# Seven products for eight in the second MoE's input product, with w_in's sums kept in DRAM

## The chip, the cores and the metric

The kernel runs on one core of one Trainium2 chip. The metric is the device time of one execution in microseconds: the median of three runs is 862.21 us before the change (861.88 to 862.39). Lower is better. The engines are named as the profile names them: PE is TensorE (PEld its weight loads), DVE is VectorE, ACT is ScalarE, POOL is GpSimd, and SP is SyncE, which here issues all DMAs.

## The reference, cut to what matters

Causal attention in blocks of 64 over 4 batches, 8 heads and 576 positions gives 2304 tokens of 512 values. Two feed-forward parts follow. All of it is float32.

```python
def _moe_ref(x, w1, w2, w3, w_out):            # x [2304, 512], w1..w3 [512, 768]
    h = np.maximum(np.maximum(x @ w1, x @ w2), x @ w3)
    return (h @ w_out).astype(np.float32)      # [2304, 512], y below

def _moe2_ref(x, w_in, w_out):                 # x = y [2304, 512], w_in [512, 2048]
    h = x @ w_in
    g = h * np.cos(h)
    return (g @ w_out).astype(np.float32)      # w_out [2048, 512]
```

## The kernel before, in words

Every product after the scores is made exact enough by splitting both operands into a high and a low part (`hi` is the value rounded to `fp32r`, `lo` the rest) and adding three products: high by high, high by low, low by high. A weight arrives as int64 words of a float64; `convert` (L526) turns 128x512 of them into the two parts: a DMA of 512 KB into `raw`, two scalings on ACT or DVE, three DVE instructions on `t`, a copy to `hi`, and a subtraction on DVE to `lo`.

**Stages.** The attention of 32 items (batch, half, pair of heads) runs first, with units of the first MoE fed in between (`fill`, `units`). `ahead` (L917), called from item 10 on, converts weights of the second MoE early and keeps the two parts in DRAM (`kept_in`, `kept_out`). After the attention the rest of the first MoE runs alone. Its results `y` go by `hm` tiles to DRAM, and `split_y` (L1016) reads them back and splits them.

**The second MoE** goes over five chunks of tokens (four of 512, one of 256) and 16 column tiles of w_in. `hstage` (L1043) makes one tile of h: 12 matmuls into one PSUM bank `psm` (four blocks of 128 of the inner dimension, three products each), then on DVE a cosine's range reduction in two instructions (`th`), the sine on ACT, a multiplication on DVE, and the split into `gh` (copy on ACT) and `gl` (subtraction on DVE). `ostage` (L1065), two tiles later, multiplies `gh` and `gl` by a tile of w_out into the output banks `po` (up to four, one for each 128 tokens): three matmuls of 512 columns for each. Four banks hold `psm` tiles in this part (two of `ps_m`, two of `ps_h`) and four hold `po`. w_in and w_out stay in SBUF, high and low, from the first chunk on.

**What sets the order.** `Plan` records every operation, prices it, and lists it in time order by its own costs, forward and backward in turn (L309, L389). Each engine then runs its instructions strictly as listed. An operation's `lead` makes it due earlier. Copies and subtractions can be given to more than one engine. Pools are opened and closed as operations: what lies in `wc` and `wk2` (L1038: the tiles of the second MoE's inner work) can be used only after `moe` and `wk` are closed, that is when every user of the first MoE's tiles is done, the DMA of the last `hm` to DRAM among them. All of it is recorded by one helper, so every instruction has the line L214 in the profile; the names of the tiles tell them apart.

Of the kernel before, what the change touches and what calls it, by code (L numbers as in the profile page):

```python
# [8 lines left out]
F32 = mybir.dt.float32  # L9
# [120 lines left out]
class Plan:  # L130
# [176 lines left out]
    HOLD = {"SP": 20000.0}  # L307

# [158 lines left out]
def fused_kernel(tc, qk, qk4, q1, k1, v2, w1, w2, w3, wout, w_in2, w_out2, out):  # L467
# [58 lines left out]
    def convert(src, hi, lo, pool, bufs):  # L526
# [10 lines left out]
        R.vector.tensor_tensor(i32(t), i32(t), add, ALU.add)  # L537
        R.copy(hi, t)
        R.sub(lo, t, f32(hi))

# [252 lines left out]
    def pv(*its):  # L793
# [119 lines left out]
    NA = 6  # L913
    AHEAD = [("in", fc) for fc in range(NA, NFC)] + [("out", fc) for fc in range(3, NFC - 1, 3)]
    kept = {}

    def ahead():  # L917
        if len(kept) < len(AHEAD) and converted[0] == 4 * NFF:
            kind, fc = AHEAD[len(kept)]
            both = cv.tile([P, 2, 512], F32R, "both", tag="raw", bufs=CVR)  # L920
            convert(w_in2[fc] if kind == "in" else w_out2[:, fc], both[:, 0], both[:, 1], cv, CVR)
            kept[kind, fc] = dram.tile([P, 2, 512], F32, f"kept_{kind}{fc}")
            R.sync.dma_start(kept[kind, fc], f32(both))
# [31 lines left out]
    for n in range(NI + 1):  # L955
# [23 lines left out]
        if n > 9 and n % 3:  # L979
            ahead()  # L980
# [4 lines left out]
    chunks = [(t, min(CH, NT - t)) for t in range(0, NT, CH)]  # L985
# [4 lines left out]
    wih, wil, woh, wol = {}, {}, {}, {}  # L990
    raw_from = [0]

    def conv(kind, fc, pool, src):
        w = pool.tile([P, 2, 512], F32R, f"w_{kind}{fc}")
        if (kind, fc) in kept:
            R.sync.dma_start(f32(w), kept[kind, fc])
        else:
            raw_from[0] += 1
            convert(src, w[:, 0], w[:, 1], (cv, wb)[raw_from[0] % 2], 2)
        return w  # L1000

    def conv_in(fc, pool):
        w = conv("in", fc, pool, w_in2[fc])
        wih[fc], wil[fc] = ([w[:, i, k * P:(k + 1) * P] for k in range(NK)] for i in range(2))

    def conv_out(fc, pool):
        w = conv("out", fc, pool, w_out2[:, fc])
        woh[fc], wol[fc] = w[:, 0], w[:, 1]

    yh, yl = {}, {}  # L1010

    def alloc_y(pool, c, tag):
        yh[c] = [pool.tile([P, CH], F32R, f"yh{tag}_{k}", tag=f"yh{tag}_{k}") for k in range(NK)]
        yl[c] = [pool.tile([P, CH], F32R, f"yl{tag}_{k}", tag=f"yl{tag}_{k}") for k in range(NK)]

    def split_y(c, k):  # L1016
        t0, n = chunks[c]
        raw = cv.tile([P, 512], F32, "t", tag="t", bufs=4)
        for p, frm, to, m in pieces(t0, n):
            R.sync.dma_start(raw[:, to:to + m], y_dram[p][k][:, frm:frm + m])  # L1020
        R.copy(yh[c][k][:, :n], raw[:, :n])
        R.sub(yl[c][k][:, :n], raw[:, :n], f32(yh[c][k][:, :n]))

    alloc_y(wb, 0, "0")
    for k in range(NA):
        if fill:
            fill.pop(0)[1]()
        conv_in(k, wb)
        if k < NK:
            split_y(0, k)  # L1030
        if fill:
            fill.pop(0)[1]()
    while fill:
        fill.pop(0)[1]()
# [4 lines left out]
    wk2 = R.open(moe, name="wk2", bufs=1)  # L1039
    TWO_PI = 2.0 * math.pi  # L1040
    g = {}

    def hstage(c, fc):  # L1043
        n = chunks[c][1]
        ps = bank()[:, :n]
        prods = [(wih[fc], yh[c]), (wih[fc], yl[c]), (wil[fc], yh[c])]
        for k in range(NK):
            with R.unit():
                for i, (w, x) in enumerate(prods):
                    R.tensor.matmul(ps, w[k], x[k][:, :n], start=(k == 0 and i == 0),  # L1050
                                    stop=(k == NK - 1 and i == 2))
        t = wk2.tile([P, CH], F32, "th", tag="t", bufs=3)[:, :n]
        gh = wk2.tile([P, CH], F32R, "gh", tag="gh", bufs=3)[:, :n]
        gl = wk2.tile([P, CH], F32R, "gl", tag="gl", bufs=3)[:, :n]
        R.vector.tensor_scalar(i32(t), ps, 1.0 / TWO_PI, 0.25, ALU.mult, ALU.add)
        R.vector.scalar_tensor_tensor(t, i32(t), -TWO_PI, ps, ALU.mult, ALU.add)
        R.scalar.activation(t, t, AF.Sin, bias=halfpi)
        R.vector.tensor_tensor(t, ps, t, ALU.mult)
        R.copy(gh, t)
        R.sub(gl, t, f32(gh))  # L1060
        g[c, fc] = (gh, gl)

    banks = {}

    def ostage(c, fc):  # L1065
        t0, n = chunks[c]
        gh, gl = g.pop((c, fc))
        for t in range(n // P):
            if fc == 0:
                banks[c, t] = ps_o.tile([P, DM], F32, "po", tag=f"O{t}")  # L1070
            ts = slice(t * P, (t + 1) * P)
            prods = [(gh, woh[fc]), (gh, wol[fc]), (gl, woh[fc])]
            with R.unit():
                for i, (a, w) in enumerate(prods):
                    R.tensor.matmul(banks[c, t], a[:, ts], w, start=(fc == 0 and i == 0),
                                    stop=(fc == NFC - 1 and i == 2))
            if fc == NFC - 1:
                o = wk2.tile([P, DM], F32, "osb", tag="osb", bufs=2)
                R.copy(o, banks[c, t])
                R.sync.dma_start(out[t0 + t * P:t0 + (t + 1) * P, :], o)  # L1080

    LAG = 2
    seq = [(c, fc) for c in range(len(chunks)) for fc in range(NFC)]
    for n in range(len(seq) + LAG):
        if n < len(seq):
            c, fc = seq[n]
            if c == 0:
                conv_out(fc, wc)
                while len(wih) < min(NFC, NA + 1 + fc * (NFC - NA) // (NFC - 2)):
                    conv_in(len(wih), wc)  # L1090
            if fc == 4 and c + 1 < len(chunks):
                alloc_y(*((wk2, c + 1, "1") if c % 2 == 0 else (wb, c + 1, "0")))
            if 8 <= fc < 8 + NK and c + 1 < len(chunks):
                split_y(c + 1, fc - 8)
            hstage(c, fc)
        if n >= LAG:
            ostage(*seq[n - LAG])
    last = ()
    for p in (ps_h, ps_o, wk2, wc, wb, edge, dram, ps_m, cv, const):
        R.close(p, *last)  # L1100
        last = (p,)
# [63 lines left out]
```

## Time and profile before

| what | value |
|---|---|
| median of three runs | 862.21 us |
| profiled execution: span, first to last instruction | 859.3 us |
| PE busy | 852.3 us (99%) |
| DVE busy | 569.0 us (66%) |
| ACT busy | 446.3 us (52%) |
| DMA | 96.91 MB, mean 113 GB/s |

The page gives the profiled execution's span and no other time of it; 2.9 us lie between that span and the median of the runs. Busy times are sums over one engine; an engine that is busy nearly all the time sets the pace, and the others matter where it waits for them. A matmul's duration in these rows is longer than its share of the engine, because matmuls overlap: the distance between the starts of two neighbours is what one costs.

### The profile page before, as it was taken

The page shows a single profiled execution, that of the slowest core. Times are in us where ns is not written, and L with a number is a line of the kernel's source. Part 1 is how long each engine was busy: PE and PEld are TensorE (multiplying, and loading weights), DVE is VectorE, ACT ScalarE, POOL GpSimd, SP SyncE. Part 2 cuts the span into 40 slices and gives each one's busy share as a digit, 9 for nine tenths or more (in the row PEclk, how much of TensorE's full clock was granted, in tenths as well). Part 3 has the DMA queues.
Part 4 walks back from the last instruction along what each step waited for, and adds up shares of the span by engine and source line. Part 5 has one row for each costly group of instructions (what it writes and reads, how often), then busy time and mean ns, then how long its engine had stood idle before and what let it go on. Part 6 is the DMA issues. An engine that isn't in the chain of part 4 may idle for free.

```text
span 859.3 us, 12728 instructions
## 1 busy us (share of the span) xinstructions
PE 852.3 (99%) x4674; PEld 714.3 (83%) x4674; DVE 569.0 (66%) x1157; ACT 446.3 (52%) x1002; POOL 5.6 (1%) x38
## 2 busy tenths in 40 slices
PE   8999999999999999999999999999999999999998
PEld 7788888888888888888899888888888888888897
DVE  7999999569865598358144989455645564555454
ACT  7997999658775598434224444322332232322233
POOL 2000000000000000000000000000000000000000
PEclk9999999999999999999999999999999999999999
DMA  7655666446643367342125811200011001100000
GB/s 274 214 184 180 219 190 207 132 152 211 227 139 120 111 190 231 140 176 92 48 82 182 342 76 37 74 25 0 1 53 47 0 1 39 36 0 1 25 26 25
DMA packets 47006, 96.91 MB, mean 113 GB/s; under 512 B 6240, under 2 KB 18528, under 8 KB 46944
## 3 DMA queue, kind: packets, MB, share of 16 engines
q1 hardware_dynamic: 46944, 96.10, 33.9%
q8 instruction: 37, 0.61, 0.3%
q14 instruction: 25, 0.20, 0.1%
HBM read 75.63 MB, written 20.45 MB: 112 GB/s over the span
## 4 chain that ended last, share of the span: by engine, by line
PE 90%; DVE 6%; ACT 3%; issue 1%; POOL 0%; DVEq 0%; ACTq 0%; POOLq 0%
PE psm L214 55%; PE po L214 23%; PE tb L214 5%; PE X L214 3%; PE SA L214 2%; PE SB L214 2%; DVE top L214 1%; DVE t L214 1%; ACT prob L214 1%; ACT other L214 1%; DVE hm L214 0%; DVE m2high L214 0%; ACT pt L214 0%; DVE wlo L214 0%; DVE qh L214 0%
## 5 line engine op out<-in xcount | busy, mean ns | idle before, releaser
L214 PE MATMUL psm<-yh,w_in 128*128 128x512 f32 (+1 forms) x640 | 194.4, 368 | 0.0
L214 PE MATMUL po<-w_out,gh 128*128 128x512 f32 x576 | 177.6, 390 | 0.0
L214 ACT ACTIVATE th<-th,halfpi 128x512 f32<-128x512 f32 (+1 forms) x80 | 54.5, 682 | 186.3 <-DVE th L214 186.2
L214 PE MATMUL psm<-xhi,whi 128*128 128x512 f32 (+1 forms) x360 | 135.9, 378 | 0.0
L214 PEld LDWEIGHTS psm<-yh,w_in 128*128 128x128 f32 x640 | 117.1, 188 | 20.6
L214 PE MATMUL psm<-xhi,wlo 128*128 128x512 f32 (+1 forms) x360 | 132.9, 369 | 0.0
L214 PE MATMUL psm<-xlo,whi 128*128 128x512 f32 (+1 forms) x360 | 132.8, 369 | 0.0
L214 PEld LDWEIGHTS po<-w_out,gh 128*128 128x128 f32 x576 | 107.1, 188 | 21.4
L214 PE MATMUL psm<-yl,w_in 128*128 128x512 f32 (+1 forms) x320 | 117.7, 368 | 0.0
L214 PE MATMUL po<-w_out,gl 128*128 128x512 f32 x288 | 112.0, 389 | 0.0
L214 DVE TENSOR_SCALAR th<-psm 128x512 int32<-128x512 f32 (+1 forms) x80 | 51.0, 637 | 73.7 <-PE psm L214 67.6
L214 DVE TENSOR_TENSOR th<-psm,th 128x512 f32<-128x512 f32 (+1 forms) x80 | 51.0, 637 | 51.7 <-ACT th L214 51.6
L214 PEld LDWEIGHTS psm<-xhi,wlo 128*128 128x128 f32 x360 | 67.9, 189 | 11.8
L214 PEld LDWEIGHTS psm<-xhi,whi 128*128 128x128 f32 x360 | 67.9, 189 | 9.4 <-ACT kh L214 0.2
L214 PEld LDWEIGHTS psm<-xlo,whi 128*128 128x128 f32 x360 | 68.0, 189 | 8.9
L214 DVE TENSOR_TENSOR gl<-th,gh 128x512 fp32r<-128x512 f32 (+1 forms) x80 | 50.9, 636 | 35.1 <-ACT gh L214 34.3
L214 DVE TENSOR_TENSOR hm<-psm,hm 128x512 f32<-128x512 f32 (+1 forms) x60 | 37.9, 632 | 54.6 <-PE psm L214 49.4
L214 ACT CAST gh<-th 128x512 fp32r<-128x512 f32 (+1 forms) x77 | 44.4, 576 | 55.1 <-DVE th L214 55.1
L214 PEld LDWEIGHTS psm<-yl,w_in 128*128 128x128 f32 x320 | 60.3, 188 | 10.6
L214 PEld LDWEIGHTS po<-w_out,gl 128*128 128x128 f32 x288 | 54.0, 188 | 11.4
L214 PE MATMUL tb<-ident,prob 128*128 128x128 f32 x374 | 53.6, 273 | 1.6 <-ACT pt L214 1.0
L214 ACT COPY pt<-tb 128x512 f32<-128x512 f32 (+3 forms) x88 | 49.7, 586 | 8.1 <-PE tb L214 7.7
(132 smaller groups left out, 1338.3 us busy)
## 6 DMA issues: line engine op xcount, KB each, us to landing
raw<-w SPq DMA_DIRECT2D x18, 512.0 KB, 4.0
raw<-w_in SPq DMA_DIRECT2D x16, 512.0 KB, 4.2
raw<-w_out SPq DMA_DIRECT2D x16, 512.0 KB, 4.8
k<-k SPq DMA_DIRECT2D x24, 288.0 KB, 3.1
vr<-v SPq DMA_DIRECT2D x16, 320.0 KB, 3.9
q<-q SPq DMA_DIRECT2D x20, 256.0 KB, 2.8
kept_in<-both SPq DMA_DIRECT2D x10, 512.0 KB, 3.6
w_in<-kept_in SPq DMA_DIRECT2D x10, 512.0 KB, 7.6
```

The costliest lines, as they stand in the source:

```text
L214: return lambda: getattr(real, method)(*[value(a) for a in args], **{k: value(a) for k, a in kw.items()})
```

## The change

The tokens go in three blocks `s` of two times 384, w_in's column tiles in eight pairs (j, j+8), and the inner dimension in two halves of 256. A stage (s, j) is then a product of a 2x2 by a 2x2 block matrix, and it is made with seven block products for eight (Strassen's algorithm in a form with shared sums). One block product is six matmuls of 384 columns (two blocks of 128 of the inner dimension, three products each).

- **Sums of w_in.** `pair_sums` makes them once on DVE for each pair: four additions or subtractions of 256 columns. `keep_pair` splits four tiles (three of 512 and one of 256 columns) and writes both parts to DRAM. `load_pair` reads them back for every stage, three stages ahead; w_in no longer stays in SBUF. `convert` is cut into `whole` and `split` for this.
- **Sums of y.** `split_y` makes, for each block and each of two k, four sums on DVE and seven splits, into 18 rotating tiles `y0` to `y17`, of which one block uses 14.
- **The stage.** Three PSUM tiles A, Bk and C take the seven products. Between two products into the same tile the value so far is read out, by ACT (`ha`, `hh`) or by additions on DVE (`hu`, `hv`, `ha`); the next product then adds to what is in the bank. `psm` has only the two banks of `ps_m`, because six banks now hold `po`. The cosine part reads h from SBUF.
- **w_out.** Even pairs stay in SBUF, odd ones are loaded for each block. Only tiles 9, 11 and 13 are kept ahead of time.
- **Order.** `ahead` is called from item 17 on and takes whole pairs, and the first eight items' product of probabilities and v gets a lead of 10000 ns.

```diff
+    EARLIER, FIRST_ITEMS = 10000.0, 8
...
             R.unit_op.cost += R.SWITCH
+            if its[0].n < R.FIRST_ITEMS:
+                R.unit_op.lead = R.EARLIER
...
+    def pair_sums(j):
+        x, y = (whole(w_in2[fc], cv, CVR) for fc in (j, j + HALF))
+        a, b = (cv.tile([P, 512], F32, "t", tag="t", bufs=4) for _ in range(2))
+        one, two = slice(0, QUARTER), slice(QUARTER, 2 * QUARTER)
+        R.vector.tensor_tensor(a[:, one], y[:, one], y[:, two], ALU.add)
+        R.vector.tensor_tensor(a[:, two], a[:, one], x[:, one], ALU.subtract)
+        R.vector.tensor_tensor(b[:, one], x[:, one], y[:, one], ALU.subtract)
+        R.vector.tensor_tensor(b[:, two], x[:, two], a[:, two], ALU.subtract)
+        return x, a, b, y[:, two]
+
+    def keep_pair(j):
+        for n, t in enumerate(pair_sums(j)):
+            both = cv.tile([P, 2, 512], F32R, "both", tag="raw", bufs=CVR)[:, :, :t.n]
+            split(both[:, 0], both[:, 1], t)
+            kept["in", j, n] = dram.tile([P, 2, t.n], F32, f"kept_in{j}_{n}")
+            R.sync.dma_start(kept["in", j, n], f32(both))
...
-        if n > 9 and n % 3:
+        if n > 16 and n % 3 and len(AHEAD) > 3:
             ahead()
...
-    ps_h = R.open(ps_x, name="ps_h", bufs=1, space=PSUM, side="right")
-    bank_pools.append((ps_h, 2))
...
+    def split_y(s):
+        parts7 = [[y_tile() for k in range(2)] for _ in range(7)]
+        for k in range(2):
...
+            put(0, r[0, 0])
+            R.vector.tensor_tensor(a, r[0, 1], r[0, 0], *sub)
+            R.vector.tensor_tensor(b, r[1, 1], a, *sub)
+            put(1, b)
+            put(2, r[1, 0])
+            R.vector.tensor_tensor(r[0, 1], r[1, 1], r[0, 1], *sub)
+            put(3, r[0, 1])
+            put(4, a)
+            R.vector.tensor_tensor(r[1, 0], r[1, 0], b, *sub)
+            put(5, r[1, 0])
+            put(6, r[1, 1])
...
+        A, Bk, C = (bank()[:, :TK] for _ in range(3))
+        a, u, v, h = tile("ha"), tile("hu"), tile("hv"), tile("hh")
+        product(0, A, True)
+        R.copy(a, A)
+        product(1, Bk, True)
+        R.vector.tensor_tensor(u, Bk, a, ALU.add)
+        product(2, A, False)
+        R.copy(h, A)
+        product(3, Bk, False)
+        R.vector.tensor_tensor(v, Bk, a, ALU.add)
+        product(4, C, True)
+        R.vector.tensor_tensor(v, C, v, ALU.add)
+        product(5, Bk, False)
+        R.vector.tensor_tensor(a, Bk, a, ALU.add)
+        product(6, C, False)
+        R.vector.tensor_tensor(u, C, u, ALU.add)
+        for f, x, t in ((j, 0, h), (j + HALF, 1, v), (j + HALF, 0, a), (j, 1, u)):
...
+            R.vector.tensor_scalar(i32(c), t, 1.0 / TWO_PI, 0.25, ALU.mult, ALU.add)
+            R.vector.scalar_tensor_tensor(c, i32(c), -TWO_PI, t, ALU.mult, ALU.add)
+            R.scalar.activation(c, c, AF.Sin, bias=halfpi)
+            R.vector.tensor_tensor(c, t, c, ALU.mult)
+            split(gh, gl, c)
...
+            hstage(s, j)
+            if n + 3 < len(seq):
+                pairs[n + 3] = load_pair(n + 3)
+            if n + 1 < len(seq):
+                load_out(*seq[n + 1])
+            if j == HALF - 1 and s + 1 < NS:
+                ys[s + 1] = split_y(s + 1)
```

**Where the order moves.** Three places matter below. In these rows `psm`, `po` and the other names carry a running number, so that two numbers are two tiles.

PE, where the second MoE begins, before: the last w_in product ahead of the first w_out products. Three more tiles of 12 matmuls, into three other banks, stand ahead of these rows, and nothing of the second MoE's w_out.

```order
L214 MATMUL psm_5489<-yl0_3_4859,w_in3_4772 128x512
L214 MATMUL psm_5489<-yh0_3_4846,w_in3_4772 128x512
L214 MATMUL po_5513<-w_out0_5454,gh_5499 128x512 x2
L214 MATMUL po_5513<-w_out0_5454,gl_5507 128x512
L214 MATMUL po_5520<-w_out0_5454,gh_5499 128x512 x2
L214 MATMUL po_5520<-w_out0_5454,gl_5507 128x512
```

PE at the same place after the change: the last matmul of the first MoE, and the first products of stage (0, 0), with `psm_5585` as Bk, `psm_5601` as A and `psm_5647` as C. `pair0` to `pair2` lie in `wb`, `pair3` in `wc`.

```order
L214 MATMUL psm_5536<-hh_5495,vlo5_1946 128x256
L214 MATMUL psm_5585<-y2_5236,pair1_5332 128x384 x3
L214 MATMUL psm_5585<-y3_5374,pair1_5332 128x384 x3
L214 MATMUL psm_5601<-y0_5176,pair0_5308 128x384 x3
L214 MATMUL psm_5601<-y1_5305,pair0_5308 128x384 x3
L214 MATMUL psm_5601<-y4_5266,pair0_5308 128x384 x3
L214 MATMUL psm_5601<-y5_5402,pair0_5308 128x384 x3
L214 MATMUL psm_5585<-y6_5226,pair2_5349 128x384 x3
L214 MATMUL psm_5585<-y7_5411,pair2_5349 128x384 x3
L214 MATMUL psm_5647<-y8_5209,pair1_5332 128x384 x3
L214 MATMUL psm_5647<-y9_5355,pair1_5332 128x384 x3
L214 MATMUL psm_5585<-y10_5294,pair3_5610 128x384 x3
```

Before, four tiles in four banks needed nothing of the pool `wc`; now two products do, and the third adds to a bank that must first be copied into a tile of `wc`.

DVE at the same place after the change, from its first instruction of the second MoE's stages on (`out0` and `out8` are tiles of w_out, `t` is one in conversion).

```order
L214 TENSOR_TENSOR hu_5619<-psm_5585,ha_5608 128x384
L214 TENSOR_TENSOR out0_5612<-t_5357,out0_5612 128x512
L214 TENSOR_TENSOR out8_5621<-t_5510,out8_5621 128x512
L214 TENSOR_SCALAR th_5645<-hh_5636 128x384
L214 TENSOR_TENSOR hv_5653<-psm_5585,ha_5608 128x384
L214 SCALAR_TENSOR_TENSOR th_5645<-th_5645,hh_5636 128x384
L214 TENSOR_SCALAR t_5643<-t_5643 128x512
L214 TENSOR_TENSOR hv_5653<-psm_5647,hv_5653 128x384
L214 SCALAR_TENSOR_TENSOR t_5643<-raw_5573,t_5643 128x512
L214 TENSOR_TENSOR th_5645<-hh_5636,th_5645 128x384
L214 TENSOR_TENSOR ha_5608<-psm_5585,ha_5608 128x384
```

Before, DVE's first instructions here were the cosine's on `psm_5412`, mixed with w_out's subtractions; now four of the eleven rows (`hu`, `hv` twice, `ha`) read a bank to which a later product waits to write, and the conversions stand between them.

PE in the middle of the second MoE, before: the end of one w_in tile, and the w_out products of an earlier one.

```order
L214 MATMUL psm_6321<-yl1_3_5991,w_in6_5464 128x512
L214 MATMUL psm_6321<-yh1_3_5974,w_in6_5464 128x512
L214 MATMUL po_6193<-w_out4_5580,gh_6295 128x512 x2
L214 MATMUL po_6193<-w_out4_5580,gl_6300 128x512
L214 MATMUL po_6201<-w_out4_5580,gh_6295 128x512 x2
L214 MATMUL po_6201<-w_out4_5580,gl_6300 128x512
```

PE in the middle of the second MoE, after: one stage of block 1, with `psm_7031` as Bk, `psm_7019` as A and `psm_7064` as C.

```order
L214 MATMUL psm_7031<-y17_6832,pair1_6790 128x384 x3
L214 MATMUL psm_7019<-y0_6690,pair0_6781 128x384 x3
L214 MATMUL psm_7019<-y1_6811,pair0_6781 128x384 x3
L214 MATMUL po_7046<-out0_5612,gh_6936 128x512 x2
L214 MATMUL po_7046<-out0_5612,gl_6950 128x512
L214 MATMUL psm_7031<-y2_6708,pair2_6824 128x384 x3
L214 MATMUL psm_7031<-y3_6835,pair2_6824 128x384 x3
L214 MATMUL psm_7064<-y4_6719,pair1_6790 128x384 x3
L214 MATMUL psm_7064<-y5_6792,pair1_6790 128x384 x3
L214 MATMUL po_7046<-out8_5621,gh_6999 128x512 x2
L214 MATMUL po_7046<-out8_5621,gl_7009 128x512
L214 MATMUL psm_7031<-y6_6738,pair3_6861 128x384 x3
```

Before, a tile of h was left alone once it was made; now a stage comes back to the same bank three times, with a w_out group or another product in between.

## Rows read from the trace of the kernel before

**Rows 1.** The page, busy time of each engine and PE's granted clock in 40 slices.

```profile
PE 852.3 (99%) x4674; PEld 714.3 (83%) x4674; DVE 569.0 (66%) x1157; ACT 446.3 (52%) x1002; POOL 5.6 (1%) x38
...
PEclk9999999999999999999999999999999999999999
```

**Rows 2.** What PE waited for: us in total, times, longest; the first of five.

```profile
PE psm L214 <- POOL ident L214: 1.4, 1, 1.4
```

**Rows 3.** Stretches: us, busy of PE, PEld, DVE, ACT, POOL, PE's clock, DMA, GB/s.

```profile
300.00:357.00 57.00, 57.00 (x409) 47.66 (x409) 44.08 (x88) 44.94 (x104) 0.00 (x0) 1.00 0.56 181
357.00:420.00 63.00, 63.00 (x279) 52.13 (x280) 35.29 (x62) 23.47 (x44) 0.00 (x0) 1.00 0.37 126
420.00:462.00 42.00, 42.00 (x321) 40.68 (x320) 13.26 (x29) 9.77 (x22) 0.00 (x0) 1.00 0.19 66
462.00:473.00 11.00, 11.00 (x52) 9.14 (x51) 5.90 (x10) 6.48 (x10) 0.00 (x0) 1.00 0.96 334
473.00:805.00 332.00, 332.00 (x1467) 274.90 (x1466) 198.34 (x307) 107.47 (x171) 0.00 (x0) 1.00 0.13 47
```

**Rows 4.** Groups by shape: names, shapes, count, busy us, mean ns, idle before.

```profile
L214 PE MATMUL psm<-yh,w_in 128*128 128x512 f32 x512 | 168.9, 389 | 0.0
...
L214 PEld LDWEIGHTS psm<-yh,w_in 128*128 128x128 f32 x640 | 117.1, 188 | 20.6
...
L214 PE MATMUL psm<-yh,w_in 128*128 128x256 f32 x128 | 25.5, 282 | 0.0
```

**Rows 5.** The chain that ended last: start us, us, engine, tile, instructions.

```profile
478.75 2.72 PE psm L214 x12
481.48 2.72 PE po L214 x12
...
805.15 1.43 PE psm L214 x12
```

**Rows 6.** DVE and ACT by shape, columns as in rows 4.

```profile
L214 DVE TENSOR_TENSOR th<-psm,th 128x512 f32<-128x512 f32 x64 | 44.2, 690 | 42.3 <-ACT th L214 42.2
...
L214 DVE TENSOR_SCALAR t<-t 128x512 int32<-128x512 int32 x56 | 23.4, 417 | 4.5 <-ACT t L214 4.3
...
L214 ACT COPY pt<-tb 128x384 f32<-128x384 f32 x19 | 8.7, 475 | 3.0 <-PE tb L214 3.0
...
L214 DVE TENSOR_TENSOR th<-psm,th 128x256 f32<-128x256 f32 x16 | 6.8, 424 | 9.4 <-ACT th L214 9.4
```

**Rows 7.** Timeline at 742 us, one hand-over: start, us, instruction, idle before.

```profile
742.21 0.39 PE L214 MATMUL psm<-yh,w_in 128*128 128x512 f32 x1
...
742.63 0.69 DVE L214 TENSOR_SCALAR th<-psm 128x512 int32<-128x512 f32 x1 [1.11 <-PE psm L214]
743.36 0.69 DVE L214 SCALAR_TENSOR_TENSOR th<-th,psm 128x512 f32<-128x512 int32 x1
...
744.14 0.72 ACT L214 ACTIVATE th<-th,halfpi 128x512 f32<-128x512 f32 x1 [3.34 <-DVE th L214]
```

**Rows 8.** Timeline where the second MoE begins: PE, ACT and SP.

```profile
462.25 0.40 PE L214 MATMUL psm<-yh,w_in 128*128 128x512 f32 x1
...
462.49 0.37 ACT L214 COPY hm<-psm 128x256 f32<-128x256 f32 x1 [1.83 <-PE psm L214]
...
462.76 1.66 ACT L214 CAST w_out<-t 128x512 fp32r<-128x512 f32 x3
462.89 0.32 SPq L214 DMA_DIRECT2D y<-hm  x1
```

**Rows 9.** The same place: DVE, and ACT's table load.

```profile
466.18 0.69 DVE L214 TENSOR_SCALAR th<-psm 128x512 int32<-128x512 f32 x1 [6.02 <-DMA y<-hm]
466.79 0.68 DVE L214 TENSOR_TENSOR w_out<-t,w_out 128x512 fp32r<-128x512 f32 x1
467.39 0.68 DVE L214 SCALAR_TENSOR_TENSOR th<-th,psm 128x512 f32<-128x512 int32 x1
...
468.14 1.28 ACT L214 ACT_TABLE_LOAD   x1 [1.70 <-DVE th L214]
```

More of the change, by code (lines that the diff above doesn't have):

```diff
@@ L982, in fused_kernel @@
     R.close(at)
[L985 removed]
+    TK = 384
+    NS = NT // (2 * TK)
     wb = R.open(at, name="wb", bufs=1, side="right")
     ps_o = R.open(ps_x, name="ps_o", bufs=1, space=PSUM, side="right")
[L988 to L1000 removed]
@@ L1016, in split_y @@
[L1016 to L1032, printed above, removed]
@@ L1033, in fused_kernel, with load_pair @@
-    while fill:
-        fill.pop(0)[1]()
+    GROUPS = (512, 512, 512, QUARTER)
+    def load_pair(n):
+        where = {}
+        for x, w in enumerate(GROUPS):
+            if n == 0 and x == 3:
+                continue
+            pool, bufs = (wc, 3) if x == 3 else (wb, 1) if n % 3 == 0 else (wc, 2)
+            t = pool.tile([P, 2, w], F32R, f"pair{x}", tag=f"pair{x}", bufs=bufs)
+            R.sync.dma_start(f32(t), kept["in", n % HALF, x])
+            where[x] = t
+        return where
@@ L1035, in fused_kernel @@
+    ys = {0: split_y(0)}
+    pairs = {0: None}
+    while AHEAD or fill:
+        if AHEAD:
+            ahead()
+            if 0 in pairs and pairs[0] is None and ("in", 0, 3) in kept:
+                pairs[0] = load_pair(0)
+        for _ in range(2):
+            if fill:
+                fill.pop(0)[1]()
     R.close(wk)
@@ L1038, in fused_kernel @@
     wc = R.open(moe, name="wc", bufs=1)
-    wk2 = R.open(moe, name="wk2", bufs=1)
     TWO_PI = 2.0 * math.pi
[L1041 to L1080, printed above, removed]
@@ L1082, in fused_kernel, with load_out @@
-    LAG = 2
-    seq = [(c, fc) for c in range(len(chunks)) for fc in range(NFC)]
+    woh, wol, g, banks = {}, {}, {}, {}
+    def load_out(s, j):
+        stays = j % 2 == 0
+        if stays and s:
+            return
+        for fc in (j, j + HALF):
+            slot = f"out{fc}" if stays else f"out{j % 4}_{fc // HALF}"
+            w = wc.tile([P, 2, 512], F32R, slot, tag=slot)
+            if ("out", fc) in kept:
+                R.sync.dma_start(f32(w), kept["out", fc])
+            else:
+                convert(w_out2[:, fc], w[:, 0], w[:, 1], cv, CVR)
+                if not stays:
+                    kept["out", fc] = dram.tile([P, 2, 512], F32, f"kept_out{fc}")
+                    R.sync.dma_start(kept["out", fc], f32(w))
+            woh[fc], wol[fc] = w[:, 0], w[:, 1]
@@ new lines, in ostage @@
+    def ostage(s, j):
+        for x in range(2):
+            for t in range(TK // P):
+                n = x * (TK // P) + t
+                if j == 0:
+                    banks[n] = ps_o.tile([P, DM], F32, "po", tag=f"O{n}")
+                ts = slice(t * P, (t + 1) * P)
+                for f in (j, j + HALF):
+                    gh, gl = g[s, f, x]
+                    with R.unit():
+                        for i, (a, w) in enumerate([(gh, woh[f]), (gh, wol[f]), (gl, woh[f])]):
+                            R.tensor.matmul(banks[n], a[:, ts], w, start=(f == 0 and i == 0),
+                                            stop=(f == NFC - 1 and i == 2))
+                if j == HALF - 1:
+                    o = wc.tile([P, DM], F32, "osb", tag="osb", bufs=2)
+                    R.copy(o, banks[n])
+                    r0 = 2 * TK * s + n * P
+                    R.sync.dma_start(out[r0:r0 + P, :], o)
@@ L1084, in fused_kernel @@
+    LAG = 1
+    seq = [(s, j) for s in range(NS) for j in range(HALF)]
+    pairs[0][3] = wc.tile([P, 2, QUARTER], F32R, "pair3", tag="pair3", bufs=3)
+    R.sync.dma_start(f32(pairs[0][3]), kept["in", 0, 3])
+    for n in range(1, 3):
+        pairs[n] = load_pair(n)
+    load_out(0, 0)
     for n in range(len(seq) + LAG):
         if n < len(seq):
[L1086 to L1090, printed above, removed]
```

81 lines of the change are left out of this document (56 added, 25 removed).

## The prediction

> **What bounds the kernel now.** I read busy times first: PE works 852.3 of the 859.3 us of the span, at full clock in all 40 slices [rows 1]. Then PE's waits: the longest of five is 1.4 us at the start, and the five together are 3.3 us [rows 2]. Some 3 us at the end are the last copy and store. So the time is the sum of PE's work, and I price it from the chain of waits: there every group of 12 matmuls of 512 columns takes 2.72 us, 226.7 ns each, w_in's (`psm`) as well as w_out's (`po`), and a group of 12 of 256 columns takes 1.43 us, 119.2 ns each [rows 5]. The reader should see that the 389 ns of the table by shape [rows 4] are durations of overlapping matmuls and price nothing. Last the stretches [rows 3]: in the second MoE's even part (473 to 805 us) DVE works 198.3 of 332.0 us and ACT 107.5, so both have room.
>
> The profiled execution's span is 859.3 us; the median of the runs is 862.2. I take the 2.9 us between them as unchanged and make the sum against 862.2.
>
> **PE's columns.** Before, a chunk of 512 tokens takes 12 matmuls for each of 16 tiles, over four chunks 64 groups, and the last chunk 16 groups of 256 columns; the counts 512 (two of three products) and 128 [rows 4] agree. 64 x 2.72 + 16 x 1.43 = 197.0 us. After, 24 stages of 7 products of 6 matmuls are 1008 matmuls of 384 columns. No row has that width in this form, but it lies midway between 256 and 512, so (226.7 + 119.2) / 2 = 172.9 ns, and 1008 x 0.1729 = 174.3 us. **Saved: 22.7 us.** The w_out part keeps its 864 matmuls, and PE's part up to the first w_in product is the same set of instructions.
>
> **Where the second MoE begins.** Before, PE goes from the first MoE to the second at 462.25; I count from there. ACT's copy of the last y starts at +0.24 and takes 0.37, its store is issued at +0.64, and DVE's first `th` can start only at +3.93, let go by that store [rows 8, 9]. PE did not feel it: four tiles in four free banks, 4 x 2.72 = 10.9 us, stood in between. Now only two products (2 x 6 x 0.173 = 2.08 us) need nothing of `wc`. The third adds to A, and A must first be copied to `ha`, a tile of `wc`. The copy starts at 3.93 and takes 0.48 (128x384 from PSUM, [rows 6]); the third product starts at 4.45. First loss: 2.4 us. Behind this wait stand w_out's casts on ACT, w_out's subtractions and the first cosine on DVE, and on SP all loads of `pair` tiles for the stages 1 and 2.
>
> From there I walk on with hand-overs of 0.19 us from PE to DVE (742.21 + 0.23 = 742.44, start 742.63) and 0.09 from DVE on (744.05 to 744.14) [rows 7]. A DVE instruction of 512 columns holds its engine 0.60 us (starts 466.18, 466.79, 467.39, [rows 9]); 690 ns at 512 and 424 at 256 [rows 6] make 557 ns and a turn of 0.47 at 384; the cheap form (417 ns) has turns of 0.33 and 0.27. ACT makes two w_out casts and a scaling ahead of its copy of A to `hh`, so the fifth product (C, in A's bank) starts at 6.7 instead of 6.5. DVE has the first tile's cosine ahead of `ha`, and that waits for ACT's table load (1.28 us, [rows 9]) and sine; so Bk's bank is free for the next stage's first product at 10.6 instead of 10.0. `pair3`, needed by the sixth product at 7.7, is issued at 3.95, the first of the loads of `wc`; the store next to it took 3.3 us to let DVE go. By 12.3 us PE has done 42 + 6 products' matmuls and one w_out group, 9.0 us of work. **Lost: 3.3, taken as 3.7 us** for the pieces I rounded down. Bounds: 2.4, the first loss alone; 9, if the loads, which share the queue at 334 GB/s here [rows 3], come late for the sixth product and for the second stage.
>
> **One stage.** PE: 42 x 0.1729 + 36 x 0.2267 = 15.4 us. DVE: 17 instructions of 0.47 and 4 of 0.27 make 9.1 us, 59%. The hand-overs: a product ends, 0.19, the reading 0.56, 0.09, together 0.84 us, or about 0.82 over ACT's copy, and there is always another product (1.04 us) and in three of five cases a w_out group (0.68 us) in between, as the order shows. So the slack is 0.2 us at ACT's two and 0.9 at DVE's three. It is nothing if the reader is free. I take 0.04 us a stage, **1 us**; the bound above is a rival. Below nothing it can't go, since PE has no waits there to lose.
>
> **Block 0 and the borders.** In block 0 DVE also converts some 11 tiles of w_out (0.33 + 3 x 0.60 = 2.1 us each, 23.5) and makes the sums and splits of block 1 (22 x 0.47 = 10.3): 8 x 9.1 + 33.8 = 107 of 123 us, 86%. Ten of the 14 new y tiles take the place of old ones that the stage before the border still reads. So between the `hu` of stage (0, 7) and that of (1, 0) stand 32 DVE instructions, 28 x 0.47 + 4 x 0.27 = 14.2 us, beside 17.1 us of PE (five products, 12 w_out groups, three products, one group). It fits with little to spare, twice. **Lost: 2 us**, with 0 and 10 as bounds.
>
> **Ahead of it.** The sums of w_in cost DVE some 2.3 us a pair more (four instructions of 256 columns, 1.4, and splits of 1792 columns for 1024, 0.9), 18 in all, and block 0's y another 8. From 300 to 462 us DVE stands idle 12.9 + 27.7 + 28.7 = 69 us [rows 3], and PE stays busy through all three; I cost it at nothing. If that cover were gone, it is 26 us of DVE, not of PE. The earlier product of probabilities and v can win at most the 1.9 us of PE's waits that are not the first [rows 2], or lose as much; nothing, with both ends kept. The DMAs of `pair` tiles, 1.8 MB each 15.4 us, are 114 GB/s against 334 seen.
>
> **The sum.** 862.2 - 22.7 + 3.7 + 1 + 2 = 846.2, **846 us**.
>
> [...] The gaps are short, so 4 in 100.
>
> **Rival, DVE late.** DVE takes its instructions as listed: w_out's subtraction waited until 466.79 behind `th`, though its cast belongs to ACT's run that ended at 464.42 [rows 8, 9]. [...] So one late reading holds all behind it. If in block 0 and at the borders the bounds above are reached (10 for 2), and the beginning costs 5 for 3.7: 855 us; the band is 850 to 860. For it: 86%. Against it: from 300 to 357 us DVE was busy 44.1 of 57.0 us, 77%, beside a PE that never stopped [rows 3], and the order gives each reading a product of slack. 20 in 100.
>
> **Rival, slower than before: two banks.** Every hand-over has the reader one or two instructions late. With one (0.5 us) ACT's two lose 0.3 each, 0.6 x 24 = 14 us: 860. With two (1.1 us), ACT's lose 0.5 and DVE's three 0.2 each, 1.6 x 24 = 38 us: 862.2 - 22.7 + 3.7 + 38 = 881 us. It turns slower than before from (22.7 - 3.7) / 24 = 0.79 us a stage. Against it: 59% and 0.9 us of slack. 8 in 100.
>
> **Rival, no gain from fewer columns.** A weight load takes 188 ns [rows 4]; were 384-column matmuls bound by it, 1008 x 0.188 = 189.5 would save 7.5 us: 861 us. The 256-column groups run at 119 ns a matmul with the same loads, so 3 in 100.
>
> **Rival, better.** The beginning costs 2.4, the rest nothing, the start gains 1: 839 to 842 us, 15 in 100.
>
> **How the numbers follow.** The forecast's own band, 842 to 850, has 50 in 100. The range from 840 to 857 leaves out the slower cases, the upper end of DVE late and a sliver below, together under 2 in 10. A measurement of this kernel tells 0.2%, 1.7 us, from no change. Faster by more: 0.88 (forecast 0.50, better 0.15, DVE late 0.19, clock 0.04). Within: 0.04 (loads, some of two banks). Slower: 0.08.
>
> **What the profile will show.** Right: groups of six `psm` matmuls in 1.04 us; PE idle 3 to 5 us between the last `hh` matmul and the second stage, first for ACT's `ha` behind the store of y; stages 15.4 to 15.6 us apart. DVE late shows as PE waits on DVE `hu`, `hv` and y tiles in block 0 and near the borders; two banks as the same waits in all 24 stages; the clock in its own column; loads as 1.13 us for six. Wrong altogether would be PE waits ahead of the second MoE, which I cost at nothing.

## The result, and the profile after

The median of the runs is 847.15 us after the change (846.43 to 847.49) and 862.05 us before it in the same session (861.82 to 862.39). The ratio is 0.9829, 95% interval 0.9815 to 0.9843. Forecast were 846.0 us and a range of 840 to 857. The profiled execution has a span of 844.7 us, for 859.3.

The page of after: busy times and granted clock, as in [rows 1].

```profile
PE 835.3 (99%) x4722; PEld 723.5 (86%) x4722; DVE 636.3 (75%) x1441; ACT 486.0 (58%) x1114; POOL 5.5 (1%) x38
...
PEclk9999999999999999999999999999999999999999
```

PE still works 99% of the span and its clock stays at 1.00 in every stretch shown below. DVE gained 67 us of work and DMA 58 MB (155.15 for 96.91 MB), and neither became the bound. The list of what PE waited for, in after (us in total, times, longest), beside [rows 2]:

```profile
PE psm L214 <- ACT ha L214: 1.4, 1, 1.4
PE psm L214 <- POOL ident L214: 1.4, 1, 1.4
...
PE psm L214 <- ACT hm L214: 0.7, 1, 0.7
...
PE psm L214 <- DVE ha L214: 0.2, 1, 0.2
```

Two of these lie in the second MoE, the one on ACT's `ha` and the one on DVE's `ha`; both are for readings of its first stage. In the 23 stages that follow PE waits for nothing. The stretches of after answer to [rows 3] (us, busy of PE, PEld, DVE, ACT, POOL, PE's clock, DMA, GB/s):

```profile
462.00:473.00 11.00, 9.38 (x57) 8.58 (x55) 5.57 (x12) 6.14 (x11) 0.00 (x0) 1.00 0.66 236
473.00:484.00 11.00, 10.98 (x58) 10.31 (x59) 11.00 (x26) 6.25 (x13) 0.00 (x0) 1.00 1.03 413
484.00:600.00 116.00, 116.00 (x579) 104.64 (x578) 105.11 (x226) 62.09 (x118) 0.00 (x0) 1.00 0.58 203
600.00:700.00 100.00, 100.00 (x504) 90.72 (x503) 67.82 (x146) 38.84 (x74) 0.00 (x0) 1.00 0.52 177
700.00:800.00 100.00, 100.00 (x498) 90.00 (x497) 69.25 (x151) 40.26 (x77) 0.00 (x0) 1.00 0.57 191
```

In block 0 (484 to 600) DVE is busy 105.1 of 116.0 us, 91%, and PE 116.0 of 116.0. The reader should see both numbers at once: DVE at 91% beside the bound cost nothing here, as what it delivered had slack (in e3_dve4, below, 43 us more of it are hidden).

Where the time went, split at the start of the first w_in matmul of the second MoE and 0.23 us (a matmul's share) after the start of the last w_out matmul:

| us | before | after | difference |
|---|---|---|---|
| up to the first w_in matmul | 462.25 | 463.53 | +1.3 |
| second MoE | 393.28 | 377.21 | -16.1 |
| after the last w_out matmul | 3.80 | 3.91 | +0.1 |
| span | 859.33 | 844.65 | -14.7 |

The chain of waits of after, one stage in the middle (start us, us, engine, tile, instructions), as in [rows 5]:

```profile
644.48 1.06 PE psm L214 x6
645.55 0.70 PE po L214 x3
646.25 2.10 PE psm L214 x12
648.35 0.70 PE po L214 x3
649.05 2.10 PE psm L214 x12
651.15 0.70 PE po L214 x3
651.85 2.10 PE psm L214 x12
653.95 6.16 PE po L214 x27
660.11 1.06 PE psm L214 x6
```

From 644.48 to 660.11 is one stage: 42 `psm` and 36 `po` matmuls in 15.63 us, all PE. Forecast were 15.42 of columns and 0.04 of hand-overs. The 0.19 us above the columns is in no list of waits. It sits in the runs themselves: 27 `po` matmuls take 6.16 where 27 x 226.7 ns is 6.12, and 3 take 0.70 where it is 0.68. In [rows 5] the `po` run that follows a `psm` run of the same width takes exactly 2.72. In before's second MoE the width changes in one place, its last chunk; there the `po` run after the `psm` run of 256 columns at 805.15 [rows 5] takes 2.75 (chain of waits of before):

```profile
806.59 2.75 PE po L214 x12
```

So the suspicion was that each change of width costs some 0.02 us, and e8_width below tests it.

The beginning of the second MoE in after, the timeline of PE and ACT (start us, us, instruction, idle before), beside [rows 8, 9]:

```profile
463.53 2.25 PE L214 MATMUL psm<-y,pair 128*128 128x384 f32 x12
463.73 0.37 ACT L214 COPY hm<-psm 128x256 f32<-128x256 f32 x1 [0.66 <-PE psm L214]
...
466.69 0.48 ACT L214 COPY ha<-psm 128x384 f32<-128x384 f32 x1 [2.58 <-DMA y<-hm]
...
467.22 5.59 PE L214 MATMUL psm<-y,pair 128*128 128x384 f32 x30 [1.43 <-ACT ha L214]
...
473.02 1.31 PE L214 MATMUL psm<-y,pair 128*128 128x384 f32 x6 [0.21 <-DVE ha L214]
```

This is the wait that the prediction named, on the tile that it named, behind the store of y. Third product at +3.69 us (forecast 4.45), second stage's first product at +9.49 (10.6), first w_out group over at +11.34 (12.3). With 48 x 0.1733 and 0.70 of work in it, 9.0 us, about 2.3 us are lost in place of 3.3. The list of waits has only 1.64 of them (1.43 and 0.21). The rest shows in the starts of the matmuls: after each stop the first matmul takes 0.28 us to the next start for 0.17, and the one before the stop counts as busy for 0.16 us beyond its share. So each of the two listed waits cost PE some 0.27 us more than the list says.

### The profile page after: what moved, and what is told of

Read it like the earlier page. It is cut to its first block, busy times and chain, and to the rows that moved or that the text cites. A ratio compares the mean times of both kernels' runs of the same rounds, so it can differ in the third digit from the quotient of the medians.

```text
span 844.7 us, 13582 instructions
## 1 busy us (share of the span) xinstructions
PE 835.3 (99%) x4722; PEld 723.5 (86%) x4722; DVE 636.3 (75%) x1441; ACT 486.0 (58%) x1114; POOL 5.5 (1%) x38
## 2 busy tenths in 40 slices
DMA packets 68627, 155.15 MB, mean 184 GB/s; under 512 B 8528, under 2 KB 26960, under 8 KB 68560
## 4 chain that ended last, share of the span: by engine, by line
PE 95%; DVE 2%; ACT 2%; DMA 0%; issue 0%; POOL 0%; ACTq 0%; POOLq 0%
PE psm L214 56%; PE po L214 23%; PE tb L214 6%; PE X L214 4%; PE SB L214 3%; PE SA L214 3%; DVE top L214 1%; ACT other L214 0%; ACT prob L214 0%; DVE t L214 0%; DMA y<-hm 0%; ACT pt L214 0%; DVE pt L214 0%; DVE prob L214 0%; DVE other L214 0%
## 5 line engine op out<-in xcount | busy, mean ns | idle before, releaser
L214 PE MATMUL psm<-y,pair 128*128 128x384 f32 x1008 | 192.4, 337 | 1.6 <-ACT ha L214 1.4
L214 PEld LDWEIGHTS psm<-y,pair 128*128 128x128 f32 x1008 | 179.0, 188 | 10.7 <-ACT ha L214 1.8
L214 PE MATMUL po<-out,gh 128*128 128x512 f32 x576 | 178.5, 391 | 0.0
L214 PEld LDWEIGHTS po<-out,gh 128*128 128x128 f32 x576 | 106.9, 188 | 16.1
L214 PE MATMUL po<-out,gl 128*128 128x512 f32 x288 | 113.1, 393 | 0.0
L214 ACT ACTIVATE th<-th,halfpi 128x384 f32<-128x384 f32 x96 | 58.6, 617 | 72.4 <-DVE th L214 72.0
L214 ACT COPY pt<-tb 128x512 f32<-128x512 f32 (+2 forms) x100 | 58.4, 605 | 15.3 <-PE tb L214 15.0
L214 PEld LDWEIGHTS po<-out,gl 128*128 128x128 f32 x288 | 54.0, 187 | 11.5
L214 ACT CAST gh<-th 128x384 fp32r<-128x384 f32 x94 | 47.4, 510 | 27.6 <-DVE th L214 26.9
L214 DVE TENSOR_TENSOR gl<-th,gh 128x384 fp32r<-128x384 f32 x96 | 51.9, 553 | 2.2 <-ACT gh L214 1.2
```

The costliest lines, as they stand in the source:

```text
L214: return lambda: getattr(real, method)(*[value(a) for a in args], **{k: value(a) for k, a in kw.items()})
```

## The experiments

The theory: the gain is PE's columns, less one wait at the start of the second MoE, less 0.2 us a stage for changes of width; DVE and the loads are hidden. Rivals: the readings of the banks or DVE eat part of the gain where no list of waits shows it; the sums of w_in, made ahead, cost the +1.3 us; the start costs more than its listed wait.

**e1_six: one product less.** Part left out: the seventh block product, so that one quarter of h lacks a term.

```diff
-        product(6, C, False)
```

> The seventh block product of every stage is left out (its sum is read all the same), so one quarter of h is wrong; the instructions of DVE, ACT and the DMAs stay. If PE's columns set the time, 24 x 6 x 0.1733 = 25.0 us go: 847.2 - 25.0 = 822 us (820 to 824), stages 14.6 us apart. If hand-overs between PE and DVE or DVE's own work set the stages, less than half of it goes: above 835 us.

Measured: 823.79 us (822.65 to 825.94), ratio to before 0.9563 (0.9549 to 0.9578). The second MoE takes 352.49 us, 24.72 less than in after (it begins at 465.50, 2.0 us later, so less of it shows in the time). 144 matmuls less at 173.3 ns are 25.0 us. A stage is 14.59 us, still 0.19 above its columns (36 x 0.1733 + 36 x 0.2267 = 14.40). A product is worth its columns in full, so PE alone sets the pace of a stage.

**e2_eight: eight products, the staging kept.** No sums of w_in or y, eight plain products, each tile of h copied from its bank.

```diff
-        return x, a, b, y[:, two]
+        return x, y
...
-    GROUPS = (512, 512, 512, QUARTER)
+    GROUPS = (512, 512)
...
+        for f, x, name in ((0, 0, "ha"), (1, 0, "hu"), (0, 1, "hv"), (1, 1, "hh")):
+            ps, t = bank()[:, :TK], tile(name)
+            product(w4[f][0], y7[2 * x], ps, True)
+            product(w4[f][1], y7[2 * x + 1], ps, False)
+            R.copy(t, ps)
```

> Strassen undone, the staging kept: three blocks of two times 384 tokens, pairs of w_in tiles read from DRAM for every stage, two psm banks, the cosine from SBUF, but eight plain products and no sums. If the gain is the eighth product, PE has 144 matmuls of 384 columns more: 847.2 + 25.0 = 872 us (869 to 875), that is some 10 us above the kernel before, which is the price of the staging alone. If the gain came from something else in the change (the staging, the order, the lead), it stays below 860 us.

Measured: 867.12 us (866.17 to 868.04), ratio 1.0067 (1.005 to 1.0084). The chain of waits of e2_eight, in the middle:

```profile
645.71 8.20 PE po L214 x36
653.92 8.34 PE psm L214 x48
662.26 8.20 PE po L214 x36
```

One stage is 16.55 us with two changes of width and only 0.07 above its columns (48 x 0.1733 + 36 x 0.2267 = 16.48). Its second MoE takes 397.16 us, which is 24 such stages: nothing is lost at the start. This closes the account of the change. From 397.16 to after's 377.21 are 19.95 us. The 144 matmuls less (25.0), reduced by six more changes of width a stage (24 x 0.12 = 2.9) and by 2.3 at the start, make 19.8. So the time stays below the expected 869 us: the undoing brings back some 5 us less than the columns alone, because the two losses of the seven products go with them. Against the kernel before (393.28), e2_eight's narrower matmuls cost 3.9 us: 1152 x 0.1733 = 199.7 us of columns for 197.0, and 24 x 0.07 = 1.7 of changes of width for some 0.4 in before's last chunk.

**e3_dve4, e3_dve8: more work for DVE.** Four or eight additions of 384 columns more in a stage (`range(1)`, `range(2)`).

```diff
+            for extra in range(2):
+                R.vector.tensor_tensor(c, t, t, ALU.add)
```

> Four more DVE instructions of 384 columns in every stage (an addition into the cosine's tile that is overwritten), 4 x 0.47 = 1.9 us: DVE has 11.0 of 15.6 us a stage, and in block 0 some 122 of 125 us. If DVE is off the path, 847 to 850 us. If DVE is late as it is, the 24 x 1.9 = 45 us go through: 870 us or more.

> Eight more DVE instructions of 384 columns in every stage: DVE has 12.9 of 15.6 us a stage, and in block 0, with w_out's conversions and the sums of y, 8 x 12.9 + 34 = 137 of 125 us. By the working of the prediction blocks 1 and 2 still hide it and block 0 does not: 12 us more, 857 to 864 us, with PE waiting for DVE in block 0 alone. If DVE is late in every stage, 890 us; if there is room even in block 0, 848 us.

Measured: 847.65 us with four (ratio 0.9837, 0.9818 to 0.9857), 854.69 with eight (0.9919, 0.9899 to 0.9939). With four the second MoE takes 376.76 us against after's 377.21: 43 us more of DVE (679.3 for 636.3) are hidden whole. With eight it takes 383.85, +6.6 us, half of what was expected. The waits of PE in e3_dve8, and its stretch of block 0:

```profile
PE po L214 <- DVE gl L214: 1.9, 2, 1.5
...
PE psm L214 <- DVE hv L214: 1.2, 2, 0.8
```

```profile
484.00:600.00 116.00, 113.70 (x557) 100.25 (x556) 115.83 (x255) 57.43 (x111) 0.00 (x0) 1.00 0.51 178
```

Here is what DVE late looks like: DVE busy 115.8 of 116.0 us, and PE's waits on the reading `hv` that the prediction named and on the split `gl`. After has neither. The listed waits in the second MoE grew by 3.2 of the 6.6 us. Counted by the starts of the matmuls, PE is stopped 15 times for 8.4 us in all, in after three times for 2.3, and this makes 6.1 of the 6.6. The last five of the 15 lie between 580 and 608 us, around the first border between blocks, the other ten before 489.

**e4_no_lead, e5_y_store, e6_both: the start and what lies ahead of it.** e4 takes the lead from the first items' product; e5 puts the last y into a tile of another pool, so that `wc` need not wait for its store; e6 does both.

```diff
-    EARLIER, FIRST_ITEMS = 10000.0, 8
+    EARLIER, FIRST_ITEMS = 10000.0, 0
...
-            yt = wk.tile([P, CH], F32, "hm", tag="hm", bufs=3)[:, :n]
+            yt = (cv.tile([P, 512], F32, "t", tag="t", bufs=4) if sum(parts[c]) == NT else
+                  wk.tile([P, CH], F32, "hm", tag="hm", bufs=3))[:, :n]
```

> The lead of the first eight items' product of probabilities and v is taken away, nothing else. PE came 1.3 us later to the second MoE than before the change (463.53 for 462.25 us). If the lead is its cause, that point goes back to about 462.3 and the time to 846 us. If DVE's added sums of w_in are, it stays within 0.4 us, at 847.2. If the lead brought something that the sums took, it goes to 464 or more, 848 us or more.

> The last chunk's y tiles lie in the pool cv and not in wk, so that the pools of the second MoE's inner work can open without waiting for their store to DRAM. If that store is what PE loses its time on there, the third product starts some 0.8 us after the second ends instead of 1.6 and pair3 comes earlier: PE's wait on ha falls from 1.4 to 0.6 us, and the time to 845 to 846.5 us. If the loads of the pair tiles or DVE's first readings are next in line, PE waits as long a product or two later and the time stays at 847.2.

> The last chunk's y tiles in the pool cv and no lead for the first items, together. If the two gains seen apart (1.6 us and 1.9 us, each on another chip than the changed kernel's own runs) are real and of different places, 843.7 us (843.2 to 844.5). If the order of the part ahead of the second MoE just falls out differently with every change of the plan, the lead's share is chance, and it is 845.2 us (844.5 to 846.5).

Measured: e4 845.48 us (845.33 to 846.04; ratio 0.9814, 0.9801 to 0.9827), e5 845.19 (844.97 to 845.45; 0.9808, 0.9795 to 0.9822), e6 845.20 (844.76 to 845.64; 0.9809, 0.9794 to 0.9824). In e5 ACT's copy no longer waits for the store, and the 12 matmuls and the next 24 run on with no wait that the list shows:

```profile
463.58 6.72 PE L214 MATMUL psm<-y,pair 128*128 128x384 f32 x36
...
464.83 0.48 ACT L214 COPY ha<-psm 128x384 f32<-128x384 f32 x1
...
466.90 3.08 PEld L214 LDWEIGHTS psm<-y,pair 128*128 128x128 f32 x18 [0.35 <-DVE hu L214]
```

The run is not quite unbroken: by the starts of the matmuls PE still loses 1.0 us in the first products, in three short stops, the first of them where the weight load waits for DVE's `hu`. The second MoE takes 375.79 us, 1.42 less than after, the size of the wait on `ha` (1.43). That term is shown. The lead is not a second one. Without it the second MoE begins at 463.34 in place of 463.53, and most of e4's gain comes from the same wait, which is half as long there (waits of PE in e4_no_lead):

```profile
PE psm L214 <- ACT ha L214: 0.7, 1, 0.7
```

The second MoE takes 376.45 us in e4, 0.76 less than after. So e4 and e5 draw on the same loss, and e6, which begins at 463.71, does not add the one to the other.

**e9_after_again: after once more.**

> The changed kernel as it is, on the chip and beside the runs of the next two: 847 us again, 846.4 to 847.5.

Measured: 846.91 us (846.60 to 847.42), ratio 0.9829 (0.9815 to 0.9844). So the 1.7 us of e5 are more than the scatter, and e5 and e6 are the fastest versions run here, with no difference between them.

**e8_width: no change of width.** The w_out products take 384 of their 512 columns, so a quarter of the output is left out; every matmul of the second MoE now has 384 columns.

```diff
-                            R.tensor.matmul(banks[n], a[:, ts], w, start=(f == 0 and i == 0),
+                            R.tensor.matmul(banks[n][:, :TK], a[:, ts], w[:, :TK], start=(f == 0 and i == 0),
```

> The second MoE's w_out products make only 384 of the 512 output columns, so a quarter of the output is left out; all matmuls of the second MoE are then equally wide. 864 x (0.2267 - 0.1733) = 46 us go in any case. In the changed kernel a run of 6 or 12 psm matmuls takes 0.02 us more than its columns, and so does a run of po matmuls. If that belongs to the change of width, runs of 12 take 2.08 us here and runs of 3 po matmuls 0.52, and a stage 13.5 us. If it belongs to the change from one bank or weight tile to another, they take 2.10 and 0.54, and a stage 13.7 us.

Measured: 798.35 us in one run. Its chain of waits, in the middle:

```profile
651.10 1.04 PE psm L214 x6
652.14 0.52 PE po L214 x3
652.66 2.08 PE psm L214 x12
...
659.94 4.68 PE po L214 x27
664.62 1.04 PE psm L214 x6
```

From 651.10 to 664.62 is 13.52 us, and 78 x 0.1733 is 13.52. The runs alternate as in after, but 12 `psm` take 2.08 and not 2.10, 3 `po` 0.52 and 27 of them 4.68, all multiples of 173.3 ns. Stages are shorter and DVE has less room in them than in after, so readings of the banks would have cost more here. The 0.19 us of after's stage is the price of eight changes of width. It does not fall at the border itself but in the first six to nine matmuls behind it. In after's blocks 1 and 2 the steps from start to start of a run of 27 `po` are on average 229, 233, 236, 224, 231, 236, 228, 232 and 231 ns and then 227 to its end, so a run of three is over before the price is paid in full. In e8_width every step is 173 or 174. What in the engine takes it, no row tells.

**e7_early, e10_n13, e11_n22: when the sums of w_in may start.** All three have e5's edit (e7 also e4's), and let `ahead` begin at item 10, 14 and 23 in place of 17.

```diff
-        if n > 16 and n % 3 and len(AHEAD) > 3:
+        if n > 22 and n % 3 and len(AHEAD) > 3:
```

> As the run before, and the conversions ahead are let in from item 10 on, as in the kernel before, and not from item 17. If the later start of the conversions costs the 1.2 us by which PE comes later to the second MoE, it begins at 462.3 us and the time is 1 us below the run before. If DVE is too full in the first 150 us, PE comes later, 464 us or more. If neither matters, it begins between 463 and 464 us.

> After with the last chunk's y in its own buffer (as in e5_y_store, 845.2 us, second MoE from 463.58), and the sums of w_in let in from the 14th step of the attention on instead of the 17th (e7_early: from the 10th, 864.6 us, second MoE from 482.6, with TensorE idle 13 us in the first 50 us against 2.5 in e6_both, before any sum ran). Theory A, sums that come early push the attention's own small steps on VectorE and ScalarE back, the more the earlier: the second MoE begins between 464 and 482, the total 846 to 864. Theory B, the plan as a whole is another one at each edit, and e7_early drew a bad one: the second MoE begins within 462.3 to 465.5 as in the eight other variants, total 844 to 847. Under both the second MoE itself takes 375.5 to 376.5.

> After with the last chunk's y in its own buffer, and the sums of w_in let in from the 23rd step of the attention on instead of the 17th: later and denser, beside the first MoE's product. If the sums cost the stretch ahead of the second MoE its 1.3 us (463.53 for 462.25 of the kernel before) because they stand in the attention, the second MoE now begins at 462.3 and the total is 843.9. If that start is the plan's scatter, it is anywhere from 462.3 to 465.5, total 844 to 847. If the sums come too late, TensorE waits for the pairs in the first stages of the second MoE, which the trace would show as PE waiting on a DMA of a pair, and the total is above 847.

Measured: 864.64 us from item 10 (863.12 to 865.30; ratio 1.0033, 1.0019 to 1.0048), 857.51 from 14 (855.69 to 858.41; 0.9948, 0.9933 to 0.9963), 845.19 from 17 (e5), 874.83 from 23 (873.52 to 876.65; 1.0147, 1.013 to 1.0164). The second MoE itself takes 375.55, 375.86, 375.79 and 376.18 us in the four. All the difference lies ahead of it: it begins at 482.56, 476.09, 463.58 and 494.78 us. The expectation that the plan's scatter is 2 us wide fell, and so did the hope for a better place. What e11_n22 named as the sign of sums that come too late, PE waiting for the load of a pair, did not show either.

Early: the stretch from 0 to 50 us in e7_early and in e10_n13 (in after PE is busy 46.71 us of it):

```profile
0.00:50.00 50.00, 36.77 (x184) 26.69 (x184) 42.55 (x122) 42.91 (x120) 5.32 (x37) 0.93 0.74 248
...
20.00:30.00 10.00, 7.74 (x33) 4.78 (x32) 10.00 (x25) 9.43 (x30) 0.00 (x0) 0.83 0.73 239
```

```profile
0.00:50.00 50.00, 42.58 (x249) 31.16 (x249) 43.09 (x135) 43.91 (x125) 5.32 (x37) 1.00 0.77 262
```

No sum runs in these 50 us; the first comes at 134.5 us in e7_early. Yet PE has run 184 matmuls where after has run 295, and what it waits for are attention's small steps on ACT and DVE, as the list of e7_early's waits shows:

```profile
PE tb L214 <- ACT pt L214: 5.0, 5, 2.4
PE psm L214 <- ACT other L214: 2.5, 2, 2.0
PE SA L214 <- ACT prob L214: 2.1, 2, 1.1
```

Another row suggests what stands in their way: one of the three `t` steps of a weight's conversion, DVE, 0 to 100 us, in after and then in e7_early.

```profile
L214 DVE SCALAR_TENSOR_TENSOR t<-raw,t 128x512 int32<-128x512 int32 x16 | 11.0, 687 | 0.0
```

```profile
L214 DVE SCALAR_TENSOR_TENSOR t<-raw,t 128x512 int32<-128x512 int32 x22 | 15.0, 681 | 0.0
```

Six more conversions stand in the first 100 us, on two engines that are nearly full there (in e7_early DVE is busy 90.0 and ACT 90.3 of these 100 us). That these hold the small steps back is argued, not shown. The early item alone is not the cost: before lets `ahead` in from item 10 as well, has 17 of these steps in its first 100 us, and PE is busy 46.79 of its first 50. Why the plan lists the conversions so early when whole pairs may come early was not tried. Of e10_n13's 12.5 us, 4.3 lie in these 50 us and 2.6 between 150 and 200.

Late: e11_n22 is undisturbed to 200 us and loses 3.5 us by 250, 5.4 from 350 to 400 and 12.1 from 400 to 462. The timeline of ACT and PE at two of its gaps:

```profile
373.42 0.68 ACT L214 ACTIVATE raw<-raw 128x512 int32<-128x512 uint32 x1 [5.08 <-DMA raw<-w_in]
376.89 0.65 ACT L214 ACTIVATE raw<-raw 128x512 int32<-128x512 uint32 x1 [2.78 <-DMA raw<-w_in]
...
378.52 0.57 ACT L214 COPY hm<-psm 128x512 f32<-128x512 f32 x1
```

```profile
379.14 0.80 PE L214 MATMUL psm<-xhi,whi 128*128 128x512 f32 x1 [5.27 <-ACT hm L214]
...
453.06 0.58 PE L214 MATMUL psm<-xhi,whi 128*128 128x256 f32 x1 [8.39 <-ACT xhi L214]
```

```profile
450.10 1.14 ACT L214 CAST both<-t 128x512 fp32r<-128x512 f32 x2 [3.13 <-DVE t L214]
452.61 0.40 ACT L214 CAST xhi<-t 128x256 fp32r<-128x256 f32 x1 [1.37 <-DMA t<-x]
```

ACT has the copy of `hm` to make, which PE waits for, but ahead of it in its list stand steps of a conversion whose data is still on the way: 5.08 and 2.78 us of waiting for a DMA, handed on to PE as 5.27. Ahead of the 8.39 us it waits 3.13 us for DVE's step `t` of a conversion, casts what came of it, and waits 1.37 us for a load of x. PE's listed waits ahead of the second MoE, without the first, sum to 22 us for 1.5 in e5_y_store. Behind the gaps the granted clock is lower too: 0.95 from 250 to 300 us, 0.76 from 380 to 390 and 0.83 from 460 to 470, means of these stretches, with PE busy all of them. Behind the gap of 5.27 us matmuls of 512 columns start 0.43 us apart from 379.74 to 384.86, and 0.23 us apart after that. By the three means it is an estimated 50 x 0.05 + 10 x 0.24 + 10 x 0.17 = 6.6 us more. DVE and ACT are far from full here (25.85 and 18.31 of 50 us from 350 to 400). It is the order that costs here, not the amount of work.

## Why the prediction was right, and where its steps were off

The time was 1.2 us off, and the second MoE, -16.1 us, was forecast at -22.7 + 3.7 + 1 + 2 = -16.0. Its parts were less exact than that:

- **PE's columns**, -22.7: a matmul of 384 columns costs 173.3 ns by e8_width's and after's chains, for a midpoint of 172.9. 1008 x 0.1733 = 174.7 against 197.0 is -22.3. Right. The rival of the weight loads is ruled out by the same row: their 188 ns do not bind.
- **Where the second MoE begins**, +3.7: measured 2.3. The mechanism was right (e5_y_store shows it) and the walk too slow, from its first step: the transfer of y took 2.46 us (464.13 to 466.59, in the chain), and `ha` could start at +3.16 for 3.93. Rounding up on top of the walk made it worse, and the sign given, PE idle 3 to 5 us there, was too long as well. The bound of 9 for late loads was far off: they went at 413 GB/s and nothing waited for them.
- **The hand-overs**, +1, and **block 0 and the borders**, +2: no wait shows for either, beyond the 0.21 us on `ha` at the end of the first stage, and e3_dve4 shows that there was room for four more DVE instructions a stage. So the rival of two banks is ruled out, and DVE late begins only between four and eight more instructions. In their place stands a cost that the prediction did not have: 0.19 us x 24 = 4.6 us for changes of width. A first measure of it could have been read ahead of time, from the 0.03 us of the last chunk of before. So the +3 was right to within 1.6 us by luck, for a reason that was not the one given; the 1.4 us too many at the start made up for most of what it lacked.
- **Ahead of it**, 0: measured +1.3, within its bound of 1.9. The sums of w_in alone are not the cause, since e2_eight makes none and begins at 463.31; the lead alone is not, since e4 begins at 463.34. Edits within the second MoE moved that point as well, to 465.50 in e1_six and 465.14 in e3_dve8. Counted by starts, the matmuls that come over 0.09 us later than is usual for their tile and width sum to 13.0 us before and 14.3 in after, 1.1 of these 1.3 us in the first 100 us, before any sum (the first is at 169 us). So PE waits a little more in the attention, under a plan that falls out otherwise at every edit; which part of the plan does it is not shown. What the prediction called hidden is hidden only where the change put it: the same sums let in six items later cost 31 us. The 69 us of idle DVE that it counted were the wrong evidence for that, so the cost of nothing was right for this plan and not in general. In e11_n22 DVE had room as well (25.85 of 50 us busy from 350 to 400), and ACT, going through its list in order, passed waits for transfers of 5.08 and 2.78 us on to PE.
- **The clock**, 0.04 among the chances: no row of before has it below 1.00, so that chance was the author's guess. After keeps 1.00 across a gap of 1.43 us. In e11_n22 the clock did fall: the stretch from 450 to 460 us, in which its gap of 8.39 us ends, has this row, where it is 0.50.

```profile
450.00:460.00 10.00, 3.26 (x11) 2.62 (x12) 3.67 (x9) 2.96 (x7) 0.00 (x0) 0.50 0.60 187
```

The measured terms: -22.3 + 2.3 + 4.2 (the changes of width, less some 0.4 that before had in its last chunk) + 1.3 + 0.1 make -14.4 beside a measured -14.7 of the span, and -14.9 between the medians.

Three sums of the prediction are off without bearing on its forecast. The hand-over of ACT's copy is 0.19 + 0.48 + 0.09 = 0.76 us by its own rows, for 0.82. A stage's `pair` tiles of 1792 KB in 15.4 us are 119 GB/s, for 114. And with two late instructions (1.1 us) ACT's two hand-overs would each lose 0.9 us by the prediction's slack of 0.2, for 0.5, so that the rival of two banks was priced some 20 us too low.

## What to carry to other kernels

Here, where PE was busy 99% of the time, removed columns were worth their full price (24.7 of 25.0 us in e1_six), and DVE beside it at 91% cost nothing while each of its results had a product of slack; test that by adding work to the engine, not by its busy share. Work that was made ahead "for nothing" was free only at its place in the engines' lists: in e11_n22 steps that waited 5.08 and 2.78 us for a transfer held back the copy behind them that PE needed, and six items of the attention decided between 845 and 875 us. And price a narrower instruction from the chain of waits, together with the places where its width meets another.

## What the runs showed of the hardware

- Where runs of 384 and of 512 columns alternate, a run costs 0.02 to 0.04 us more than its columns: 2.10 for 2.08 us, 0.70 for 0.68 and 6.16 for 6.12 in after. It falls in the first six to nine matmuls of a run, and is absent where all are of one width (e8_width). In before's last chunk, 256 beside 512 columns, it shows in the runs of 512: 2.75 for 2.72 us.
- At its two listed stops at the start of the second MoE, PE lost more than the list says: 1.43 and 0.21 us in after's list are 1.70 and 0.48 by the starts of the matmuls.
- Matmuls of 512, 384 and 256 columns cost 226.7, 173.3 and 119.2 ns apiece in a dense run (before's and e8_width's chains), so a narrower one cost more for each column: 0.443, 0.451 and 0.466 ns.
- In e7_early the granted clock was 0.83 from 20 to 30 us, where PE was busy 7.74 of 10 us and no single wait from the start to there was over 1.47 us; in after it was 1.00 from 462 to 473 us with one wait of 1.43 us and 9.38 of 11 us busy. So a clock below full was seen without a gap above 1.47 us as well.
